# Half-width stationary blocks in the attention output of a fused GLA and MLP kernel

## The chip, the core and the metric

The kernel runs on one core of one Trainium2 chip. The metric is the device time of one execution in microseconds (us), as a median over runs. The profile is of one further execution; its span goes from the first to the last instruction that the profiler recorded.

## The reference

Two layers follow each other. The first is a gated linear recurrence over 768 tokens for 4 batches and 8 heads of 48; the second is a LayerNorm, an MLP of width 384 to 1536 to 384, and a residual.

```python
# q, k, v, alpha: (4, 8, 768, 48)
for t in range(S):
    state = alpha[:, :, t, :, None] * state + einsum('bhd,bhe->bhde', k[:, :, t], v[:, :, t])
    y[:, :, t] = einsum('bhd,bhde->bhe', q[:, :, t], state)
x = y.transpose(0, 2, 1, 3).reshape(4, 768, 384)
xn = (x - mean(x)) / sqrt(var(x) + 1e-6) * g_ln
out = x + maximum(xn @ w_ch1, 0) @ w_ch2
```

## The kernel before

**Tiling.** The tokens are cut into six chunks of 128 (`c`), so there are 24 pieces of attention, one for each chunk and batch (`attention(c, b)`). All data are fp32. Heads are held as two halves `i` of four heads `p`, so a partition range of 64 (48 used) belongs to one of two heads of a pair. Within a piece the recurrence is written as matrix products: `lps` sums the logarithms of alpha (L347, L354), `tps` turns q and k (L414), `aps` are the scores k times q (L427, L442), `ups` the update of the state (L471), and `yps` is the output y (L497, L507).

**Chunk 0 and the later chunks.** In chunk 0 (`whole`) the 128 tokens are one block, the state is zero, and y is one product for each head: 128 keys against 64 queries (L497), two products for the two halves `s` of the queries. In chunks 1 to 5 each half of 64 tokens is scored by itself, and y has two parts: q against the state (`k == 0` in L505: 48 rows of `qT` are stationary, `now` or `mid` moves) and scores against v (`k == 1`: 64 rows of `at` are stationary, `vn` or `vx` moves). `s` chooses the half of the queries and so the output partitions (`halves[s]`), `j` chooses the rows, 0 to 63 or 64 to 127, and the PSUM bank `yps[j]`. In every case the moving operand has 48 elements per partition.

**TensorE tiles.** A product with at most 64 stationary columns runs on a part of the array that is 64 columns wide, at the output's partitions; one with at most 64 rows runs on a part 64 rows high. So `yps` of chunk 0 uses two tiles of 128x64, `yps`, `ups`, `aps` and `lps` of the later chunks use four tiles of 64x64, and everything else (`tps`, `xps`, the MLP) the full 128x128. Each fp32 product is two instructions of weight load (LDWEIGHTS, engine PEld in the profile) and two of MATMUL (PE), so one piece's `yps` has 64 MATMULs in a later chunk and 32 in chunk 0.

**The MLP.** Chunk 0 goes through plain products (`hidden` L590, `project` L602). Later chunks use bilinear schemes with fewer products: `hidden_product` (L892) and `product` (L714), with sums of operands made by VectorE and GpSimd.

**Order of the work.** Each part of the kernel is a Python generator, and `ORDER` is a string written out by hand that says which generator takes its next step. Engines run their own instructions in this order. The products of one `yps` stand between two `yield`s, so they are one run of TensorE instructions; what stands ahead of it and behind it is set by the string: `ups`, `aps` or `lps` of some piece, or products of the MLP.

**Readers.** `yps` is copied to `x` by ScalarE (L516, L517, L519), or by ScalarE and VectorE (L522), normalised, and turned into `xT`, the input of the MLP.

Of the kernel before, what the change touches and what calls it, by code (L numbers as in the profile page):

```python
# [60 lines left out]
def kernel(  # L61
# [36 lines left out]
    nc = tc.nc  # L98

    B, S, H, D = q.shape  # L100
# [21 lines left out]
    HS = P // 2  # L122
    halves = [slice(HS * s, HS * s + HS) for s in range(2)]
# [202 lines left out]
    def attention(c, b):  # L326
# [5 lines left out]
        cross = b % 2 and not whole  # L332
# [16 lines left out]
        else:  # L349
            a = las.pop((c, b))  # L350
            lps = ps.tile([P, 512], FP32, name="lps", tag="bank", bufs=6)
            for h in range(2):
                of = halves[1 - h if b % 2 else h]
# [29 lines left out]
        at = ats[b % len(ats)]  # L383
        if not whole:
            at = at.rearrange("k p i s t -> k (p i s t)")[:, b // 2 * NP * P:][:, :NP * P].rearrange(
                "k (p s t) -> k p s t", s=2, t=HS)
        def turned_tiles():
            turned_of[c, b] = [work.tile([R, NP, 2, HS], FP32, name=n, tag="sum", bufs=12)
                               for n in ("qT", "kT")]
            return turned_of[c, b]  # L390

        if not turned(c, b):
            qT, kT = turned_tiles()
        if turned(c, b):
# [9 lines left out]
            qT, kT = turned_tiles()  # L404
# [16 lines left out]
        if whole:  # L421
            aps = [ps.tile([P, NP, 2, HS], FP32, name=f"aps{i}", tag="bank", bufs=6)
                   for i in range(2)]
            for p in range(NP):
                for i in range(2):
                    rs = slice(64 * i, 64 * i + D)
# [3 lines left out]
                                     start=True, stop=True)  # L430
        else:
            if b % 2:
# [3 lines left out]
                for p in range(NP):  # L436
                    for s in range(2):
                        for o in range(2):
                            for i in range(2):
                                rs = slice(64 * i, 64 * i + D)  # L440
# [3 lines left out]
                                                 start=True, stop=True)  # L444
# [19 lines left out]
        vn, vx = raws["v", c, b]  # L464
# [10 lines left out]
        now, nxt = sts[b][(c + 1) % 2], sts[b][c % 2]  # L475
        mid = None if whole else work.tile([R, NP, D], FP32, name="mid", tag="mid", bufs=3)
        for s, up in enumerate(ups):
            by = gate[:R, s].unsqueeze(2).broadcast_to([R, NP, D])
            if whole:
# [10 lines left out]

        yps = [ps.tile([P, 2, NP, D], FP32, name=f"yps{r}", tag="bank", bufs=6)
               for r in range(1 if whole else 2)]
        for p in range(NP):
            if whole:
                for i in range(2):
                    for s in range(2):
                        nc.tensor.matmul(yps[0][halves[s], i, p], at[:, p, i, s], vn[:, i, p],  # L497
                                         start=True, stop=True)
                continue
            for k in range(2):  # L500
                for s in range(2):
                    for j in range(2):
                        i = j if cross else j ^ k
                        rs, hs = slice(64 * i, 64 * i + D), halves[j]
                        of, by = (qT[rs, p, s], (now, mid)[s][rs, p]) if k == 0 else (  # L505
                            at[hs, p, s], vn[hs, i, p] if s == j else vx[hs, p])
                        nc.tensor.matmul(yps[j][halves[s], i, p], of, by, skip_group_check=True,  # L507
                                         start=not (cross and k), stop=k == 1 or not cross)
        yield
        x = work.tile([P, DM], FP32, name="x", tag="row", bufs=8)  # L510
        few = work.tile([P, 5], FP32, name="few", tag="few", bufs=5)
# [2 lines left out]
        yps = [y.rearrange("t a b d -> t (a b d)") for y in yps]  # L514
# [440 lines left out]
    turns = {"YZ"[h]: first_of_chunk_0(h) for h in range(2)}  # L955
    turns |= {"PQ"[h]: second_of_chunk_0(h) for h in range(2)}
    turns |= {chr(ord("a") + n): attention(n // B, n % B) for n in range(NCB * B)}
    turns |= {chr(ord("A") + i): take_weights(i) for i in range(len(pieces))}
    turns |= {"M": mlp(), "V": hidden_products(NCB - 1), "S": combine_first(), "W": combine_weights(), "R": relus(),
# [34 lines left out]
```

## Time and profile before

| what | value |
|---|---|
| median of 3 runs | 419.16 us (416.6 to 420.09) |
| the profiled execution's own time | 417.81 us |
| its span | 416.0 us |
| instructions recorded | 11451 |
| PE busy (MATMUL) | 409.0 us, 98%, 4616 instructions |
| PEld busy (LDWEIGHTS) | 354.9 us, 85%, 4616 instructions |
| VectorE, ScalarE, GpSimd busy | 70%, 52%, 29% |
| mean granted TensorE clock | 1.000 |

PE's busy time is the union of overlapping MATMULs, whose recorded ends are modelled; a run of small MATMULs is better read from the starts, or from the steps of the chain that ended last, which go from end to end.

### The profile page before, as it was taken

The numbers are of one execution on the slowest core, as the hardware profiler recorded it, in microseconds if no ns is written. First come the engines' busy times: TensorE is split into PE (matmuls) and PEld (weight loads), VectorE is DVE, ScalarE is ACT, GpSimd is POOL, SyncE is SP. The second block draws the span as 40 slices with busy tenths as digits, with TensorE's granted clock in tenths as the row PEclk, the third lists the DMA queues.
The fourth block names the chain that finished last, engine by engine and source line by source line (L and its number), as shares of the span: only waits on it lengthen the run. The fifth ranks groups of instructions, "written<-read, shape, count | busy, mean of one in ns | idle before, by whom it ended". The sixth has DMA issues, their size and how long they took to land.

```text
span 416.0 us, 11451 instructions
## 1 busy us (share of the span) xinstructions
PE 409.0 (98%) x4616; PEld 354.9 (85%) x4616; DVE 292.8 (70%) x554; ACT 217.0 (52%) x522; POOL 122.0 (29%) x134
## 2 busy tenths in 40 slices
PE   7999999999999999999999999999999999999997
PEld 5877888876568889998889998899998889999996
DVE  3897989999997888687268973579533288125754
ACT  4787568774364576245584335773353643245110
POOL 1011013132011562144480254260236321525300
PEclk9999999999999999999999999999999999999999
DMA  8998968888878676945776868536324200000301
GB/s 263 282 272 270 283 141 282 243 169 246 230 139 229 164 151 129 237 100 140 168 144 153 200 167 213 108 45 129 109 58 120 71 1 2 19 0 25 110 20 58
DMA packets 134445, 61.26 MB, mean 147 GB/s; under 512 B 90956, under 2 KB 131276, under 8 KB 134392
## 3 DMA queue, kind: packets, MB, share of 16 engines
q1 hardware_dynamic: 133848, 60.37, 57.5%
q8 instruction: 36, 0.59, 0.6%
q10 hardware_dynamic: 544, 0.17, 0.2%
q14 instruction: 17, 0.14, 0.1%
HBM read 43.12 MB, written 17.39 MB: 145 GB/s over the span
## 4 chain that ended last, share of the span: by engine, by line
PE 94%; ACT 3%; DMA 1%; DVE 0%; issue 0%; SPq 0%; DVEq 0%
PE hps L892 32%; PE ops L714 31%; PE hps L590 8%; PE ops L602 8%; PE yps L507 5%; PE aps L442 3%; PE ups L471 2%; PE tps L414 2%; PE lps L354 2%; DMA ra<-in_alpha_dram 1%; PE aps L427 1%; PE yps L497 1%; PE xps L565 1%; ACT hT L931 0%; ACT lps L358 0%; ACT qT L418 0%
## 5 line engine op out<-in xcount | busy, mean ns | idle before, releaser
L892 PE MATMUL hps<-sum,w 128*128 128x256 f32 x192 | 46.3, 383 | 0.0
L714 PE MATMUL ops<-w,hT 128*128 128x192 f32 x224 | 40.8, 326 | 0.8 <-ACT hT L931 0.8
L892 PEld LDWEIGHTS hps<-sum,w 128*128 128x128 f32 x192 | 35.7, 190 | 6.3 <-ACT u L904 1.7
L738 ACT COPY u<-ops 128x192 f32<-128x192 f32 x30 | 9.5, 316 | 56.4 <-PE ops L714 56.3
L714 PEld LDWEIGHTS ops<-w,hT 128*128 128x128 f32 x224 | 37.2, 190 | 1.4 <-ACT hT L931 1.1
L734 POOL TENSOR_TENSOR ob<-ob,u 128x192 f32<-128x192 f32 x32 | 20.8, 659 | 56.7 <-ACT u L738 33.2
L486 POOL TENSOR_TENSOR mid<-mid,gate 112x192 f32<-112x192 f32 x20 | 14.0, 701 | 77.9 <-DVE mid L484 21.2
L590 PE MATMUL hps<-xT,w 128*128 128x256 f32 x144 | 33.9, 385 | 0.2 <-ACT few L538 0.2
L904 ACT COPY u<-hps 128x512 f32<-128x512 f32 x32 | 18.7, 585 | 28.0 <-PE hps L892 22.1
L892 PE MATMUL hps<-xT,w 128*128 128x256 f32 x136 | 33.3, 379 | 0.0
L602 PE MATMUL ops<-w,hT 128*128 128x384 f32 x96 | 32.6, 491 | 0.0
L590 PEld LDWEIGHTS hps<-xT,w 128*128 128x128 f32 x144 | 26.2, 190 | 4.2 <-ACT few L538 0.4
L904 ACT COPY hT<-hps 128x512 f32<-128x512 f32 x40 | 23.3, 585 | 12.3 <-PE hps L892 12.1
L892 PEld LDWEIGHTS hps<-xT,w 128*128 128x128 f32 x136 | 25.8, 190 | 3.4
L714 PE MATMUL ops<-ws,sum 128*128 128x192 f32 x160 | 28.6, 327 | 0.0
L602 PEld LDWEIGHTS ops<-w,hT 128*128 128x128 f32 x96 | 17.7, 190 | 11.7 <-issue 0.6
L714 PEld LDWEIGHTS ops<-ws,sum 128*128 128x128 f32 x160 | 26.4, 190 | 0.6 <-ACT few L538 0.6
L728 DVE TENSOR_TENSOR ob<-ops,ob 128x192 f32<-128x192 f32 x40 | 13.1, 350 | 16.9 <-POOL ob L734 9.5
L931 ACT ACTIVATE hT<-hT 128x512 f32<-128x512 f32 x40 | 22.9, 621 | 2.1 <-DVE hT L911 2.1
L714 PE MATMUL ops<-ws,hT 128*128 128x192 f32 x128 | 23.4, 326 | 0.0
L714 PE MATMUL ops<-more,sum 128*128 128x192 f32 x120 | 22.2, 328 | 0.0
L731 DVE TENSOR_TENSOR ob<-ob,ops 128x192 f32<-128x192 f32 x35 | 11.8, 349 | 14.0 <-PE ops L714 13.5
(223 smaller groups left out, 1037.9 us busy)
## 6 DMA issues: line engine op xcount, KB each, us to landing
ws<-in_moe_w_ch_dram SPq DMA_DIRECT2D x8, 1152.0 KB
vn<-in_v_dram SPq DMA_DIRECT2D x12, 384.0 KB
kept<-x SPq DMA_DIRECT2D x24, 192.0 KB
ob<-kept SPq DMA_DIRECT2D x24, 192.0 KB
rows<-rj SPq DMA_DIRECT2D x48, 96.0 KB
out_dram<-ob SPq DMA_DIRECT2D x18, 192.0 KB
xrows<-xt SPq DMA_DIRECT2D x64, 48.0 KB
xT<-xrows SPq DMA_DIRECT2D x16, 192.0 KB
```

The lines of the kernel that those rows point to most:

```text
L442: nc.tensor.matmul(pair[o][halves[i if o else 1 - i], p, s], k_of[rs, p, s], q_of[rs, p, s], start=True, stop=True)
L486: nc.gpsimd.tensor_mul(new, new, by)
L507: nc.tensor.matmul(yps[j][halves[s], i, p], of, by, skip_group_check=True, start=not (cross and k), stop=k == 1 or not cross)
L590: nc.tensor.matmul(hps, w1[:, f, j * P:(j + 1) * P], xT_of[0][:, f, bs], start=(f == 0), stop=(f == NF - 1))
L602: nc.tensor.matmul(ops_of[b], hT_of[c][:, j, b], w2[:, j], start=(j == 0), stop=(j == NJ - 1))
L714: nc.tensor.matmul(acc, lhs[:, j], rhs[:, j], start=j == 0 and n not in FOLLOWS, stop=j == NT - 1 and n not in FOLLOWS.values(), skip_grou ...
L728: nc.vector.tensor_add(x, acc, x)
L731: nc.vector.tensor_sub(x, x, acc)
L734: getattr(nc.vector if c + 1 == NCB else nc.gpsimd, f"tensor_{op}")(x, x, y)
L892: nc.tensor.matmul(acc[:, i], w, b, start=n not in JOINS and i == 0, stop=n not in JOINS.values(), skip_group_check=True)
L904: nc.scalar.copy(out=copied[n], in_=acc)
L931: nc.scalar.activation(out=x, in_=x, func=AFT.Relu)
```

## The change

Each stationary block of 64 queries of `yps` becomes two of 32 (`quarters`), which write 32 output partitions each. The stationary operand is cut (`of[:, o]`, `at[:, p, i, s, o]`), the moving one is the same for both. Four tiles of 128x32 are used in chunk 0, eight of 64x32 later. Nothing else is changed, `ORDER` neither.

```diff
+        quarters = [slice(u, u + HS // 2) for u in (0, HS // 2)]
+
+        def part(s, o):
+            return slice(HS * s + o.start, HS * s + o.stop)
+
         for p in range(NP):
             if whole:
                 for i in range(2):
                     for s in range(2):
-                        nc.tensor.matmul(yps[0][halves[s], i, p], at[:, p, i, s], vn[:, i, p],
-                                         start=True, stop=True)
+                        for o in quarters:
+                            nc.tensor.matmul(yps[0][part(s, o), i, p], at[:, p, i, s, o],
+                                             vn[:, i, p], start=True, stop=True)
                 continue
             for k in range(2):
                 for s in range(2):
-                    for j in range(2):
-                        i = j if cross else j ^ k
-                        rs, hs = slice(64 * i, 64 * i + D), halves[j]
-                        of, by = (qT[rs, p, s], (now, mid)[s][rs, p]) if k == 0 else (
-                            at[hs, p, s], vn[hs, i, p] if s == j else vx[hs, p])
-                        nc.tensor.matmul(yps[j][halves[s], i, p], of, by, skip_group_check=True,
-                                         start=not (cross and k), stop=k == 1 or not cross)
+                    for o in quarters:
+                        for j in range(2):
+                            i = j if cross else j ^ k
+                            rs, hs = slice(64 * i, 64 * i + D), halves[j]
+                            of, by = (qT[rs, p, s], (now, mid)[s][rs, p]) if k == 0 else (
+                                at[hs, p, s], vn[hs, i, p] if s == j else vx[hs, p])
+                            nc.tensor.matmul(yps[j][part(s, o), i, p], of[:, o], by,
+                                             skip_group_check=True,
+                                             start=not (cross and k), stop=k == 1 or not cross)
```

## The prediction

> **What bounds the kernel now.** I read the shares of the page first, then the chain that ended last, then the groups by line, and at last the timeline of single blocks.
>
> ```profile
> PE 409.0 (98%) x4616; PEld 354.9 (85%) x4616; DVE 292.8 (70%) x554; ACT 217.0 (52%) x522; POOL 122.0 (29%) x134
> ...
> PEclk9999999999999999999999999999999999999999
> ...
> PE 94%; ACT 3%; DMA 1%; DVE 0%; issue 0%; SPq 0%; DVEq 0%
> ```
>
> TensorE is the bound from about 33 us on: 94% of the chain is PE, the clock is never held back, and no wait for data stands in the chain between 33 and 332 us. A microsecond taken from `yps` there is a microsecond of the end, and one added is too. Of the 24 blocks of `yps`, all 20 of L507 lie in this stretch, and of the four of L497 three are in the chain (the step x32 at 15.76 and the step x64 at 20.30); the fourth, at 29.5, is beside a chain of ScalarE.
>
> ```profile
> L507 PE MATMUL yps<-vn,at 64*64 64x48 f32 x320 | 19.9, 218 | 0.0
> ...
> L471 PE MATMUL ups<-vn,qk 64*48 64x48 f32 x544 | 11.1, 207 | 0.0
> ...
> L497 PE MATMUL yps<-vn,at 128*64 128x48 f32 x128 | 4.3, 223 | 0.0
> ```
>
> L507 has four such groups, 1280 MATMULs; L497 has 128. The mean of 218 ns is latency and says nothing of the rate, as many are in flight. The rate is in the chain:
>
> ```profile
> 20.30 1.89 PE yps L497 x64
> ...
> 26.04 1.09 PE aps L442 x64
> ...
> 84.05 0.51 PE ups L471 x32
> 84.56 0.93 PE yps L507 x64
> ...
> 137.34 1.08 PE yps L507 x64
> ...
> 141.51 0.36 PE ups L471 x32
> ```
>
> Each line is a step of the chain: its start, its length, and how many MATMULs it merges.
>
> **Rounds.** A block of L507 has 64 MATMULs on four tiles, 16 on each. 0.93 us / 16 = 58 ns for one round, in which each tile does one weight load of 64 columns and one MATMUL of 48. `ups` (48 columns, 48 moving elements, four tiles) takes 0.36 / 8 = 45 ns a round. L497 has two tiles: 1.89 / 32 = 59 ns. Elsewhere in the chain: `aps` L442 with 64 columns and 64 elements has 0.93 for 64, 58 ns as well, so the 48 elements of `yps` are hidden behind its 64 columns; L414 (128 elements) has 0.44 / 4 = 110 ns; L714 (128 columns, 192 elements) has 1.30 / 8 = 162 ns. So a round is set by the larger of the two counts, at some 0.82 ns each and 5 ns or less beside, and the tiles run it at the same time.
>
> **Modes.** Where a block stands behind one with tiles of another size, it costs more: `yps` 1.08 behind L892 and 0.93 behind `ups`; `ups` 0.51 behind L590 and 0.36 behind `yps`. That is 0.15 us each time. The rows between 64x128 and 64x64 show that a change in columns alone is enough: `aps` L442 stands directly behind `aps` L427 and takes 1.09 where it takes 0.93 elsewhere, 0.16. Before, a `yps` behind or ahead of `ups`, `aps` or `lps` paid nothing there.
>
> **The change, part by part.**
>
> **1. Shorter rounds, in chunks 1 to 5.** The MATMULs of a block become 128, on eight tiles, again 16 on each. With 32 columns and 48 elements the larger count is 48, so I take the row of `ups`, 45 ns: 16 x 45 = 0.72 us. Four more tiles start one after the other; the timeline shows what that costs.
>
> ```profile
> 64.42 0.26 PE L507 MATMUL yps<-st,qT 48*64 48x48 f32 x2
> 64.44 0.26 PE L507 MATMUL yps<-mid,qT 48*64 48x48 f32 x2
> 64.52 0.23 PE L507 MATMUL yps<-st,qT 48*64 48x48 f32 x2
> ```
>
> The four tiles' first MATMULs start at 64.424, 64.430, 64.437 and 64.444 in the trace, some 6.5 ns apart; the second round comes 0.10 later. Four more tiles are 4 x 6.5 = 26 ns once a block. So 0.75 us for 0.93: 0.18 saved, x 20 = 3.6 us. Bounds: if the moving elements were hidden too, the 32 columns alone would give 0.82 x 32 + 5 = 31 ns, a block of 0.52, 8.2 us saved; L714, where the elements do set the round, speaks against it. If a MATMUL and its load can't start sooner behind the last than `ups` shows (0.36 / 32 = 11.2 ns), a block takes 128 x 11.2 = 1.43 us and loses 0.50, 10 us in all. No row has more than four tiles at work. I choose the first value because columns, elements and rounds are nearest to the row of `ups`, and because the burst at 64.42 shows that starts 6.5 ns apart are possible: eight of them are 52 ns, and if one such step carries both of a product's MATMULs (two rounds, 90 ns) it limits nothing.
>
> **2. Shorter rounds in chunk 0.** 64 MATMULs on four tiles of 128x32, 16 rounds of 45 ns with two more starts: 0.73 for 0.94, 0.21 saved in each of three blocks, 0.6 us. The fourth is worth nothing: the chain goes by ScalarE there.
>
> **3. New changes of mode.** I went through the order of TensorE's blocks and counted on which side of each `yps` there is a block with tiles of 64x64 (or 128x64, in chunk 0), where nothing was paid before: 14 of the 20 blocks of L507 have one, two of these on both sides (at 214.6 and 274.3; at 274.3 they are even interleaved), so 16; in chunk 0 there is one (`ups` ahead of 20.30). 17 x 0.15 = 2.5 us lost. Where neighbours are 128x128, the change was paid before and is paid now. Bounds: nothing, if 64x64 and 64x32 share a mode; 17 x 0.20 = 3.4 if I take the largest (L892 x4 takes 1.06 behind `aps` and 0.86 behind L714).
>
> **4. More instructions.** 1280 + 128 more MATMULs and as many loads, 2816 in all. On the page q8 moves 0.59 MB for TensorE's 9232, 64 bytes each, so 0.18 MB or 11 packets more. They hide in the stretches of L892, where 0.22 us pass for each two instructions, and I cost them at nothing: issue is 0% of the chain. Without that cover: 0.6% of 16 engines' 416 us over 36 packets is 1.1 us a packet, 12 us. A wait of TensorE on a semaphore took 51 ns (L442 shows 24, L507 one). The change adds none that I can see; one more a block would be 1.0 us, with TensorE's whole queue behind it.
>
> ScalarE and VectorE read the same `yps` as before, some 0.1 us sooner or later; the reads that waited longest on L507 (L516, 10.6 us in six waits) are off the chain.
>
> **The sum.** -3.6 - 0.6 + 2.5 = -1.7 us. The profiled execution took 417.81 us, its span 416.0, the 1.8 around it unchanged: 416.1. The median shown is 1.35 above that execution; on it, 419.16 - 1.7 = **417.5 us**. A measurement of this kernel tells about 1% (4.2 us) from no change, so this is within 1%. This case's own range is 415.3 to 419.
>
> A page bears on how many tiles work at once: the Trainium skill, "TensorE: Matmul & The Clock Gate", section "Part 3: Packing small matmuls", states that sixteen tiles of 32x32 ran 10.6 times as fast as one and that each further tile costs about 4 ns. By 4 ns in place of 6.5 the sum would be 0.2 us lower, an estimate. No run here shows more than four tiles; the trace has 6.5 ns.
>
> **The rivals.**
>
> *A. Eight tiles are no faster than four.* The 6.5 ns of the burst may be the price of one MATMUL with its load. Then a round of eight takes 52 ns, a block 0.86, and the sum is -20 x 0.07 - 0.6 + 2.5 = +0.5 us. Or two of the four column groups share a path for weights, 2 x 32 columns in a round: 58 ns as before, nothing saved, +2.5 us. So 419.7 to 421.7. For it: nothing shows the start of more than 64 MATMULs in 0.72 us. Against it: the two column groups of today do load at the same time.
>
> *B. No change of mode between 64x64 and 64x32.* Then -4.2 us and only chunk 0's 0.15 remains: 415.1. Against it: the 0.16 between 64x128 and 64x64.
>
> *C. Slower: TensorE doesn't start pairs of load and MATMUL sooner than `ups` shows.* Place: the 20 blocks of L507. At 11.2 ns a pair, a block is 1.43: +10 us, chunk 0 (64 x 11.2 = 0.72) still saves 0.6, the modes add 2.5: +11.9, 431.1 us. Paths for moving data that serve only four tiles would give nearly the same, two times 45 ns a round. It decides from 6.5 ns a pair, where the change is worth nothing (0.93 - 1.9 / 20 = 0.835 us / 128), and from 8.2 ns it costs over 1%. For it: 11.2 is the best lasting rate that the trace has. Against it: four tiles in 45 ns are full by their own rounds, so that rate need not be a limit, and the burst is quicker.
>
> The Trainium skill, "TensorEngine Tiling (Array Packing)", section "Instruction Overhead", goes further: about 60 cycles for each matmul, and no tiling of a dimension that is already small. Paid one after the other at 2.4 GHz that is 25 ns, and 64 more a block some 32 us in all, an estimate. The trace has a MATMUL each 14.5 ns in `yps`, so here the overhead is paid by tiles in parallel, and I give that version no more than 0.01 of C's chance.
>
> *D. The change doesn't do what it says:* 32-column blocks still take tiles 64 wide. Then 32 rounds of 45 ns for 16 of 58: +0.51 x 20 + 0.5 x 3, no new modes, +11.7, 430.9.
>
> **How the numbers follow.** Forecast 0.45, A 0.17, B 0.08, C 0.27, D 0.03. The predicted time is the forecast's, 417.5. The range reaches down to 414.5 (the forecast's lower side and B) and up to 431.5 (C and D as worked out); outside are more exposed instruction loads and larger losses. Faster by over 1% is B's half and the forecast's lower edge, should the modes be cheaper than I have them: 0.14. Slower by over 1% is C and D: 0.30. The rest, 0.56, is within 1%.
>
> **What would show it.** In the chain after: L507 x128 at 0.75 us, or 0.9 with its entry; `ups`, `aps` and `lps` next to it at 0.51, 1.08 and 0.81 where they had 0.36, 0.93 and 0.66; first and second MATMUL of one tile 45 ns apart. Blocks of L507 over 1.05 us would make the prediction wrong by C or D; 0.93 means A; no 0.15 behind `ups` means B. Waits of TensorE put down to issue inside L507 would mean that instructions come too late.

## The result, and the profile after

The changed kernel takes 453.89 us (450.86 to 458.31) against 419.62 us (416.6 to 421.1) for the kernel before on the same chip: a ratio of 1.080, 95% interval 1.075 to 1.085. The ratio leaves out the slowest of its four runs, 458.31 us; the other three have a median of 452.59. The forecast was 417.5 us, within 1%, with a range up to 431.5. The change loses some 34 us, nearly three times what the slowest case of the prediction allowed.

The page of the changed kernel: busy shares, the granted clock, and the shares of the chain that ended last by engine.

```profile
PE 425.9 (94%) x6024; PEld 367.4 (81%) x6024; DVE 294.5 (65%) x554; ACT 217.3 (48%) x522; POOL 119.8 (26%) x134
...
PEclk9999999969999999799999999999899999999999
...
q8 instruction: 47, 0.77, 0.7%
...
PE 88%; issue 5%; ACT 3%; DMA 2%; DVE 2%; SPq 0%; POOL 0%; DVEq 0%
```

PE has 1408 MATMULs more, as foreseen, but its share fell from 98% to 94%, the clock has dips that it did not have, and "issue" (time for which the profile shows no wait) is 5% of the chain, where it was 0%. The groups of `yps` (L507 is now L514, L497 now L503; the last number is idle time before them and what ended it):

```profile
L514 PE MATMUL yps<-vn,at 64*32 64x48 f32 x640 | 26.1, 213 | 5.7 <-issue 5.7
...
L503 PE MATMUL yps<-vn,at 128*32 128x48 f32 x256 | 3.6, 207 | 2.6 <-issue 2.6
```

The chain that ended last, in order of time (start, length, what):

```profile
14.88 0.82 PE yps L503 x64
...
19.16 1.49 PE yps L503 x126
20.65 2.59 issue
23.25 0.29 PE yps L503 x2
...
126.23 1.31 PE yps L514 x85
...
175.55 1.60 PE yps L514 x102
177.15 2.95 issue
180.10 1.41 PE yps L514 x92
181.51 2.00 PE hps L900 x4
183.51 20.92 PE ops L722 x120
...
225.41 1.30 PE yps L514 x85
226.71 0.51 PE ups L471 x32
```

Three things stand here. A block of L514 without a pause takes 1.31 us with its entry, where it took 1.08. Other blocks are cut by pauses of 1 to 4 us. And behind such a pause the products of the MLP are slow: L900 x4 takes 2.00 and L722 x120 takes 20.92. The same blocks in the chain before, where these lines were L892 and L714:

```profile
156.87 1.06 PE hps L892 x4
157.93 19.50 PE ops L714 x120
```

The busy time by stretch in the changed kernel shows the last two things, the pause and then the slow products:

```profile
177.15:180.10 2.95, 0.00 (x1) 0.00 (x0) 2.06 (x3) 1.40 (x3) 1.78 (x2) 0.89 0.58 116
181.51:183.51 2.00, 2.00 (x5) 1.64 (x6) 0.00 (x0) 0.49 (x1) 0.00 (x0) 0.50 0.21 31
```

(length; busy time of PE, PEld, VectorE, ScalarE, GpSimd; granted clock, DMA share, GB/s). TensorE does nothing for 2.95 us in the middle of a `yps`, and then runs at half its clock.

**What ends the pauses.** TensorE's instructions come in packets of 16384 bytes on queue q8, 256 instructions of 64 bytes. For each stretch of over 0.8 us without a start of TensorE, other than the three that wait for data (at 6, 7 and 371 us), I took from the trace its place (the last start before it), its length from start to start, the count of LDWEIGHTS and MATMULs started before it, and the number of packets that had landed when TensorE went on, the last of these among them:

```
pause at us   long   instructions before   packets   last landed at   goes on after   count - 256 x packets
  20.45       2.80         692                 2          21.88            1.37              180
  41.90       0.93        1452                 5          41.46            1.37              172
  70.34       1.62        2728                10          70.53            1.44              168
  75.37       2.24        2983                11          76.24            1.37              167
  87.07       3.99        3494                13          89.85            1.21              166
 108.20       2.51        4260                16         109.16            1.55              164
 176.95       3.15        6295                24         178.65            1.45              151
 242.06       1.22        7816                30         241.79            1.48              136
 251.47       0.87        8326                32         250.82            1.51              134
 315.44       3.13       10362                40         317.00            1.57              122
```

Each pause ends 1.2 to 1.6 us after a packet has landed, whatever its length, and begins at a count that lies on a grid of 256 (the last column drifts slowly, as TensorE's other instructions are not counted in it). With the semaphore and drain instructions of TensorE that the trace records counted too, all ten pauses begin at exactly 193 above a multiple of 256. At every other border TensorE arrives 1.64 us or more after the packet has landed, and goes on. So in the pauses TensorE has used up its instructions. The sum is 22.5 us. Two of these, at 70.34 and 108.20, the chain puts down to VectorE and ScalarE; they lie on the same grid and end in the same way, so I count them here; the filler kernel below has pauses at both counts. The pauses' length does not follow the load of the DMA engines: their share is 0.55 in the longest pause and 0.67 in one of the shortest (41.90). Whether other transfers delay a packet was not tried by itself.

### The profile page after: what moved, and what is told of

It is laid out like the page before. It is cut to its first block, busy times and chain, and to the rows that moved or that the text cites. A ratio compares the mean times of both kernels' runs of the same rounds, so it can differ in the third digit from the quotient of the medians.

```text
span 453.4 us, 14267 instructions
## 1 busy us (share of the span) xinstructions
PE 425.9 (94%) x6024; PEld 367.4 (81%) x6024; DVE 294.5 (65%) x554; ACT 217.3 (48%) x522; POOL 119.8 (26%) x134
## 4 chain that ended last, share of the span: by engine, by line
PE 88%; issue 5%; ACT 3%; DMA 2%; DVE 2%; SPq 0%; POOL 0%; DVEq 0%
PE ops L722 30%; PE hps L900 29%; PE ops L610 7%; PE hps L598 7%; PE yps L514 5%; PE aps L442 2%; PE ups L471 2%; PE tps L414 2%; PE lps L354 1%; DMA ra<-in_alpha_dram 1%; PE aps L427 1%; DMA vn<-in_v_dram 1%; PE yps L503 1%; PE xps L573 1%; DVE w L264 0%
## 5 line engine op out<-in xcount | busy, mean ns | idle before, releaser
L900 PE MATMUL hps<-sum,w 128*128 128x256 f32 x192 | 46.3, 383 | 0.0
L722 PE MATMUL ops<-w,hT 128*128 128x192 f32 x224 | 42.9, 338 | 0.8 <-ACT hT L939 0.8
L900 PEld LDWEIGHTS hps<-sum,w 128*128 128x128 f32 x192 | 35.6, 190 | 6.3 <-ACT u L912 1.7
L722 PEld LDWEIGHTS ops<-w,hT 128*128 128x128 f32 x224 | 39.5, 199 | 1.5 <-ACT hT L939 1.1
L598 PE MATMUL hps<-xT,w 128*128 128x256 f32 x144 | 36.9, 408 | 1.8 <-DVE qk L362 1.3
L610 PE MATMUL ops<-w,hT 128*128 128x384 f32 x96 | 34.3, 511 | 2.3 <-ACT xn L547 2.3
L486 POOL TENSOR_TENSOR mid<-mid,gate 112x192 f32<-112x192 f32 x20 | 12.0, 602 | 88.8 <-DVE mid L484 44.0
L598 PEld LDWEIGHTS hps<-xT,w 128*128 128x128 f32 x144 | 28.1, 204 | 6.9 <-issue 1.6
L900 PE MATMUL hps<-xT,w 128*128 128x256 f32 x136 | 33.3, 379 | 0.0
L736 DVE TENSOR_TENSOR ob<-ops,ob 128x192 f32<-128x192 f32 x40 | 13.4, 352 | 28.4 <-PE ops L722 21.9
L514 PE MATMUL yps<-vn,at 64*32 64x48 f32 x640 | 26.1, 213 | 5.7 <-issue 5.7
L610 PEld LDWEIGHTS ops<-w,hT 128*128 128x128 f32 x96 | 18.5, 199 | 14.9 <-ACT xn L547 2.4
L722 PE MATMUL ops<-ws,sum 128*128 128x192 f32 x160 | 28.6, 327 | 0.0
L900 PEld LDWEIGHTS hps<-xT,w 128*128 128x128 f32 x136 | 25.8, 190 | 3.4
L722 PEld LDWEIGHTS ops<-ws,sum 128*128 128x128 f32 x160 | 26.4, 190 | 0.6 <-ACT few L546 0.6
L514 PE MATMUL yps<-mid,qT 48*32 48x48 f32 x640 | 24.0, 216 | 2.9 <-issue 2.9
L514 PE MATMUL yps<-vx,at 64*32 64x48 f32 x640 | 24.9, 213 | 1.7 <-issue 1.7
```

The lines of the kernel that those rows point to most:

```text
L486: nc.gpsimd.tensor_mul(new, new, by)
L514: nc.tensor.matmul(yps[j][part(s, o), i, p], of[:, o], by, skip_group_check=True, start=not (cross and k), stop=k == 1 or not cross)
L598: nc.tensor.matmul(hps, w1[:, f, j * P:(j + 1) * P], xT_of[0][:, f, bs], start=(f == 0), stop=(f == NF - 1))
L610: nc.tensor.matmul(ops_of[b], hT_of[c][:, j, b], w2[:, j], start=(j == 0), stop=(j == NJ - 1))
L722: nc.tensor.matmul(acc, lhs[:, j], rhs[:, j], start=j == 0 and n not in FOLLOWS, stop=j == NT - 1 and n not in FOLLOWS.values(), skip_grou ...
L736: nc.vector.tensor_add(x, acc, x)
```

## The experiments

**Theory I** says that the instruction stream is the bound: the next packet comes some 4 us after it is asked for, one at a time, so a place that uses up a whole packet in less stops. Its rivals: **T**, that the 32-column tiles themselves pause; **P**, that eight tiles cannot work at once, which would be the longer block; and **D** against **R** on what sets that longer block, the handing out of instructions or the tiles' rounds.

**Half the products on the same tiles.** Each stationary block moves the values of two heads, in chunk 0 as well.

```diff
-        for p in range(NP):
+        for p in range(0, NP, 2):
+            two = slice(p, p + 2)
...
-                                at[hs, p, s], vn[hs, i, p] if s == j else vx[hs, p])
-                            nc.tensor.matmul(yps[j][part(s, o), i, p], of[:, o], by,
+                                at[hs, p, s], vn[hs, i, two] if s == j else vx[hs, two])
+                            nc.tensor.matmul(yps[j][part(s, o), i, two], of[:, o], by,
```

> The 32-column tiles of the change with half as many products: each stationary block multiplies the values of two heads at once (96 moving elements), so the second head of each pair gets the first one's stationary block and its output is left wrong; 11451 instructions as before. Theory I (TensorE waits for its instruction stream: two blocks of 256 instructions are held, the next is asked for when the last is entered and is usable about 4 us later): no wait of TensorE inside yps over 0.5 us; a round of eight tiles at 96 elements is 84 ns, a block 0.7 us for 0.93, modes +2.5, so 414 to 421 us. Theory T (tiles of 32 columns make the waits themselves): the waits of some 20 us stay, 435 to 450. Theory P (four column groups share two paths for moving data, which is why a block takes 1.17 us from first to last start): no waits, a round 168 ns, block 1.35, 428 to 433.

Measured: 418.05 us against 419.39, ratio 0.997 (0.993 to 1.001). No pause inside `yps` is longer than 0.5 us. On the page:

```profile
PE 407.2 (98%) x4616; PEld 350.4 (84%) x4616; DVE 293.2 (71%) x554; ACT 216.9 (52%) x522; POOL 119.1 (29%) x134
...
PEclk9999999999999999999999999999999999999999
```

T falls: the tiles are those of the change, and neither pause nor slow clock is there. P falls too: a block takes 0.758 us from first to last start, and with four tiles at a time it would be 1.35. Eight tiles of 64x32 do work at the same time. The first 32 MATMULs start in 0.32 us, and after the first round, of 107 ns, a round of the eight tiles takes 82 to 88 ns there, near the 84 expected. The other 32 take 0.44 us, 13.6 ns each or 109 ns for eight; I come back to them below.

**As many instructions on the old tiles.** The kernel before, with as many tiny products (33 columns, one moving element) added as `yps` has products, in the later chunks two for each product with the state and none for the others:

```diff
+                        for _ in range(2 if k == 0 else 0):
+                            nc.tensor.matmul(yps[j][HS * s:HS * s + 33, i, p, :1], of[:, :33],
+                                             by[:, :1], skip_group_check=True, start=True, stop=True)
                         nc.tensor.matmul(yps[j][halves[s], i, p], of, by, skip_group_check=True,
```

and one in chunk 0 in the same way.

> The kernel before, 64-column tiles, with one extra tiny product (33 columns, one moving element) for each product of yps, overwritten by the real one: as many instructions as the changed kernel (14267), no new mode. The extra products alone cost 16 rounds of 32 ns a block, 0.5 us, 11 us in all. Theory I: waits of 1 to 4 us in the densest places as in the changed kernel (the first at about 20 us), 12 to 20 us in sum, and some lost clock behind them: 440 to 458 us. Theory T: no waits, 428 to 433.

Measured: 461.45 us, ratio 1.098 (1.091 to 1.105). The time alone settles less than I had expected, since the tiny products cost more than twice what I gave them: a block is 2.08 us from first to last start for 0.9, so 23 us in 20 blocks in place of 10. The trace settles it. No 32-column tile is in this kernel, and it pauses at 692, 1452, 2728, 2983, 3494, 4260, 6295, 7816 and 10362 instructions: nine of the ten counts of the changed kernel, to the instruction. (At 8326 it has no pause over 0.5 us.) The pauses sum to 13.4 us, less than in the changed kernel; its blocks take longer, 2.08 us in place of 1.17, so the same instructions are spread over more time. The two longest, in the chain:

```profile
91.02 3.29 issue
...
321.63 1.70 issue
```

**Chunk 0 alone.** L497 changed, L507 as before.

> Only chunk 0 of the change (four 128x32 tiles), L507 as before. Theory I: one wait of 2 to 3 us in the double block at about 20 us, because 128 MATMULs and their loads pass in 1.4 us, none later; 0.6 us saved by shorter rounds: 419 to 425 us. Theory T: waits in all four blocks of chunk 0, or none at all.

Measured: 423.78 us, ratio 1.011 (1.005 to 1.017). From its chain:

```profile
19.82 0.49 PE ups L471 x16
20.31 1.52 PE yps L499 x125
21.83 3.67 issue
25.50 0.37 PE yps L499 x2
```

The one pause that was expected is there, at 692 instructions again, 3.9 us long where I had 2 to 3; it lies in the double block, and the single blocks of chunk 0 have none. The granted clock was 0.50 from 24.2, near its end, to 31.0 us. A wait of 0.34 us at 1452 instructions, in L414, is on the grid as well, though none was expected later. The single blocks are quicker, 0.68 us for 0.92 from first to last start.

**Chunks 1 to 5 alone.** L507 changed, L497 as before.

> Only chunks 1 to 5 of the change (eight 64x32 tiles), chunk 0 as before. Theory I: the waits after 40 us stay in the places where one 256-instruction block is used up within 4 us, but need not be at the same yps blocks, as the borders of the instruction blocks move by 256 instructions; 12 to 18 us of waits, 440 to 453 us. If the first wait at 20 us delays everything behind it, this is nearer 440.

Measured: 452.09 us, ratio 1.079 (1.072 to 1.085). The pauses now lie at 1195, 2471, 2726, 3237, 4003, 6038, 7559 and 10105: each is 257 less than one of the changed kernel, whose chunk 0 has 256 instructions more ahead of them, and one semaphore fewer. They sum to 19.6 us, more than the 12 to 18 expected, and the time is at the upper end of the range and not nearer 440. The two parts together (4.4 and 32.7 us) make somewhat more than the change, 34.3; the difference is within the intervals.

**Half a dose.** Only the ten blocks of odd batches.

```diff
-        quarters = [slice(u, u + HS // 2) for u in (0, HS // 2)]
+        quarters = [slice(u, u + HS // 2) for u in (0, HS // 2)] if cross else [slice(0, HS)]
```

(chunk 0 as before)

> Half a dose: only the ten blocks of odd batches in chunks 1 to 5 have 32-column blocks, 1280 instructions more than before. Theory I: waits of 8 to 13 us, at about half as many places; ten blocks 0.28 us longer and some 8 new changes of mode at 0.15, 4 us; some 3 us of slow clock behind the waits: 431 to 440 us. A cost that grows with the number of 32-column blocks alone would give half of the change's loss without chunk 0, 436.

Measured: 438.22 us against 417.42, ratio 1.048 (1.044 to 1.051). Four pauses of over 1 us, 9.9 us in sum, on the grid (residues 164, 152, 135, 121). This run doesn't tell a dose by blocks from a dose by packets, as both expectations hold.

**The borders moved by half a packet.** The changed kernel with 32 tiny products, 128 instructions, added to TensorE's idle time before the first data.

```diff
+    for _ in range(32):
+        nc.tensor.matmul(idle[:33, :1], zero[:, :33], zero[:, :1], start=True, stop=True)
```

> The changed kernel with 128 more instructions of TensorE (32 tiny products) in its idle time ahead of the first data, so that every border between blocks of 256 instructions falls half a block earlier in the work. Theory I: the counts of instructions at which TensorE waits stay on the same grid of 256 (count minus 256 times the loads done is 180 falling to 120, as in the changed kernel), so other pieces of the work are hit; the sum of waits is 20 to 34 us and the time 450 to 470 us. If the waits belonged to certain yps blocks, they would move with these, by 128 counts, and the time would stay at 454.

Measured: 452.92 us, ratio 1.084 (1.080 to 1.088). The profiled execution took 460.31 us, and of its profile only the counts are used here. Pauses at 692, 1201, 1708, 3494, 4005, 6551, 7565, 8072, 9850 and 10362, with residues 180, 177, 172, 166, 165, 151, 141, 136, 122 and 122: the grid stayed and the work moved by 128 instructions across it. With the semaphores counted, each of the ten is at 193 again. Three of the counts are old ones, seven are new. A further pause, at 5720, is off the grid (126 where the others have 193); its chain shows a transfer (`kT<-rows`). So the pauses belong to the borders of packets and not to certain blocks.

**What sets the longer block.** Three quarters of the products move 8 elements in place of 48; the last head's products move 192 and write every output.

```diff
+                            if p + 1 < NP:
+                                nc.tensor.matmul(yps[j][part(s, o), i, p, :8], of[:, o], by[:, p, :8],
+                                                 skip_group_check=True, start=True, stop=True)
+                                continue
```

> Chunks 1 to 5 with eight 64x32 tiles and as many MATMULs as in the change (128 a block, chunk 0 as before), but three quarters of them move only 8 elements, so a tile's round is set by 32 columns alone; the last quarter moves 192 and writes every output with one head's stationary block, so the output isn't the reference's. What is asked: why a block of the change takes 1.17 us from first to last start where 16 rounds of 45 ns make 0.72. Theory D (TensorE hands out one instruction each 4.1 ns once the 64 that wait in its queue are used up): the first 32 MATMULs of a block start in 0.2 us, the next 64 at about 8.2 ns each, 16.5 for each product, as in the change though the moving part is a sixth. Theory R (the tiles' rounds set it): 31 ns for eight MATMULs, about 4 ns each. The time is 440 to 460 us under both, as the waits for instructions stay.

Measured: 455.25 us, ratio 1.090 (1.086 to 1.094). The starts inside a block, in us from its first MATMUL, for the changed kernel's block at 126.16 and for this kernel's at 124.38; from the trace:

```
MATMUL           32nd   48th   64th   80th   96th  112th  128th
48 elements      0.20   0.44   0.57   0.72   0.86   1.01   1.17
8 elements       0.16   0.39   0.53   0.66   0.79    -      -
```

The first 32 MATMULs with their loads are quick, and the next sixteen come late in both, 0.23 us. From the 48th on, sixteen more take 0.133 us with 8 elements, 8.3 ns each, where R asked for 4. With 48 elements it is 0.133 to 0.167, 9.2 ns each on average. A sixth of the moving data changes the pace by a tenth. The loading of weights is not the limit either: in the first 0.16 us of the changed kernel's block 32 loads start on the same eight tiles, 5 ns apart. So R falls, and D fits: TensorE takes a load and its MATMUL in some 8.3 ns, 4.2 for each if they cost the same, once those that wait in its queue are gone. The twelve blocks of the change without a pause all show the two paces: 32 MATMULs in 0.20 to 0.21 us, then the slow ones.

D is not the whole of it. In the kernel with half the products and 96 elements, the MATMULs behind the first 32 come 13.6 ns apart, where D alone allows 8.3 and the rounds of 84 ns 10.5. What adds the rest was not tried.

## Why the prediction was wrong, point by point

The span grew by 37.4 us (416.0 to 453.4). I followed in the trace how far each later product of TensorE lags behind the same product before:

| term | forecast, us | measured, us |
|---|---|---|
| 1. rounds in chunks 1 to 5 | -3.6 | +4.9 (20 x 0.24) |
| 2. rounds in chunk 0 | -0.6 | -0.7 (3 x 0.24) |
| 3. new changes of mode | +2.5 | +2.2 (16 x 0.14) |
| 4. more instructions: pauses | 0 | +22.5 |
| 4. slow clock behind the pauses | not foreseen | some 8.5 |
| sum | -1.7 | 37.4 |

That the sum meets the span's growth to 0.1 us is luck. The pauses hold some 0.6 us of ordinary spacing between starts, and the first products of the changed kernel's profile came 0.9 us sooner (L414 at 8.31, 9.20 before, as the transfer to `ra` took 4.24 us for 5.13), so some 1.5 us are put down to no term.

**Step 4 failed, and with it the prediction.** "I cost them at nothing: issue is 0% of the chain" took the mean: 2816 instructions, 11 packets in 420 us. There were 11 packets more (47 for 36). But they are all added in the densest places, where 256 instructions now pass in 1.2 us, and what counts is the time in which one packet is used. "They hide in the stretches of L892" cannot work beyond the few hundred instructions that TensorE holds. The bound, 1.1 us a packet and 12 us in all, took a packet's time on the DMA engines for the time in which TensorE gets it. The prediction did leave room: "outside are more exposed instruction loads and larger losses". The trace before held a better number: the starts of two packets there are never closer than 3.6 us (156.30 and 159.89). In the changed kernel the shortest distance is 3.3.

The kernel before has 256 instructions in as little as 1.8 us too (at 213.3) and no pause. It was not far from one: by the same count of 193 it reaches two of its borders, at 43.3 and 141.6 us, only 1.6 and 1.9 us after the packet landed. Its longest dense stretches (starts less than 0.15 us apart) have 323 and 332 instructions. In the changed kernel pauses stand in or behind stretches of 284 to 506, and some of over 320 have none, so the length alone does not decide: where the borders of the packets fall counts too, as the shifted kernel shows. A threshold was not measured.

On this the Trainium skill, "Runtime: NRT & Kernel Launch", section "Instruction fetch mechanics", says that instructions are refilled in blocks of 16 KiB, that only two such lines are held, and that the fetch is hidden by the pace of issue. The packets and the grid of 256 agree. That it is hidden, this case refutes, with 22.5 us. The same section gives TensorE room for 2048 instructions; held ahead, they would have covered every dense stretch here, and the pauses show that fewer were.

**The clock** is a loss behind the loss. Four of the six pauses of over 2 us are followed by 1.6 to 2.8 us of lag gained at half pace: L598 starts 0.43 apart in place of 0.22 until 97.6 us, then L610 is slow until 114.8, L900 and L722 until 186.3, L722 until 322.8. In these places the trace has the granted clock at 0.50, from 90.7, 111.2, 179.4 and 319.4 us on. The other two pauses, of 2.80 us at 20.45 and 2.24 at 75.37, have no slow clock behind them, and in the filler kernel it also follows a pause of 1.77 (at 181.14), so the length alone does not decide here either. The kernel with half the products, which has no such pause, has no slow clock, and neither has the kernel before. The prediction had no such term, as its worst case had TensorE busy all the time.

**Step 1 failed in its size and its sign, for another reason than its bounds.** The round was right while the first 32 MATMULs last: eight tiles do work at once, and with 96 elements their rounds are then 82 to 88 ns, as 0.82 x 96 + 5. What was wrong is that the 6.5 ns of the burst, "eight of them are 52 ns", would last. The burst ends after 64 instructions; as I read it, these had waited in TensorE's queue. Then a MATMUL and its load take 8.3 ns with 8 elements and 9.2 with 48, and 128 of them 1.17 us in all. Rival C named this mechanism and the point from which it costs over 1%, 8.2 ns, but put the limit at 11.2 ns, from `ups`, which has no more than 64 instructions and is held by its own rounds. In the `yps` of before the four tiles' rounds, 14.5 ns for a MATMUL, hide the pace behind the burst. The estimate of some 32 us beside C comes near the loss by chance: a MATMUL with its load took 8.3 to 9.2 ns here and not 25, and most of the loss is pauses.

**Steps 2 and 3 were right.** `yps` of chunk 0 is 0.24 quicker a block (forecast 0.21). A change of mode between 64x64 and 64x32 costs what I took: `ups` behind L514 at 226.71 has 0.51, and 0.36 where it stands behind `aps`. Rival B falls. Rival A's first form had the right kind of limit with the wrong price (a block of 0.86 us); its second, a shared path for weights, does not fit loads 5 ns apart. Rival D, tiles still 64 wide, falls with the 0.758 us of the first experiment.

**Two of the signs that I named** did work. Blocks of 1.31 us are over the 1.05 that speaks for C or D, and "Waits of TensorE put down to issue inside L507 would mean that instructions come too late" is what the profile shows.

No kernel run here that computes the whole of `yps` is faster than the kernel before. Chunk 0's two single blocks gain 0.24 us each, a twentieth of a per cent, far below what a measurement tells; the blocks of the later chunks are slower even without a pause. The full change with its instructions far enough apart was not run.

## What to carry to other kernels

Splitting products into smaller tiles buys array time with instructions. Count the instructions of the densest stretch, not of the kernel: here packets of 256 never started less than 3.3 us apart, and where the work used up what TensorE held in less time, TensorE stopped. A run of more than 64 instructions went at 4 ns or more for each, though the tiles could do better. A pause in the middle of a run of products, ending 1.2 to 1.6 us after a packet of the instruction queue lands, is the sign; and each pause of over 2 us may cost a half-rate stretch behind it.

## What the runs showed of the hardware that was not expected

- Instructions for TensorE come 256 at a time, with starts at least 3.3 us apart, and where TensorE had run out it went on 1.2 to 1.6 us after a packet had landed. What asks for a packet was not measured by itself.
- Far enough into a block on eight 64x32 tiles, TensorE starts a load and its MATMUL each 8.3 ns with 8 moving elements and 9.2 with 48 (from the 48th MATMUL on), and 13.6 with 96 (from the 32nd); the first 64 instructions of a block of the change take 0.20 us, 3.2 ns each.
- Eight 64x32 tiles work at the same time: their rounds are 82 to 88 ns for 96 elements while those first 64 instructions last.
- Behind four of six pauses of 2.2 to 4 us the granted clock was 0.50, for 2 us and more of the work after them.
